# New positions for all tasks in a hand-planned attention and softplus kernel

## The chip, the cores and the metric

The kernel runs on one core of one Trainium2 chip. The metric is the device time of one execution in microseconds (us); the number given for a kernel is the median of its runs.

## The reference

Linear attention per head, a norm over each head's 64 values, and a two-layer network with softplus:

```python
# q, k, v: (8, 8, 576, 64)
kv = np.einsum('bhsd,bhse->bhde', k, v)
out = np.einsum('bhsd,bhde->bhse', q, kv)
rms = np.sqrt(np.mean(out * out, axis=-1, keepdims=True) + 1e-06)
x = out / rms * g_norm              # to 4608 tokens x 512
h = x @ w_in                        # 512 x 2048
g = np.maximum(h, 0.0) + np.log1p(np.exp(-np.abs(h)))
return g @ w_out                    # 2048 x 512, result 4608 x 512
```

The weights reach the kernel as 64-bit words and are converted on the chip.

## The kernel before, in words

Every large product is computed from three parts of each operand (a rounded main part, a scaled remainder and a correction), so one product of two 128-row tiles is three TensorE passes, all in the fp32r type.

The work has three stages that overlap:

- **Weights and attention.** The in and out weights come in 16 chunks of 128 hidden columns. Six VectorE and two ScalarE steps turn one 512 KB raw piece into fp32 (L434 to L464), and splitting into three parts takes two VectorE steps (L508 or L511, then L517) and three ScalarE steps (L501/L503, L514, L521). For the first four chunks the last VectorE step is replaced by two TensorE products, L525 and L526, with ScalarE's L529 behind. For each of the 8 batches, five groups of 64x64 products make the key-value matrix (L696), which ScalarE copies (L704). For each of 36 token tiles: the q tile is transposed (L776 and L783, later on VectorE, L751), multiplied with the key-value matrix (L720, 16 products of 64x64), squared (ScalarE L793), summed (VectorE L724), rooted (POOL L727 and L728), scaled (VectorE L732), transposed again (TensorE L738 and ScalarE L802 for the first 12 tiles) and stored to DRAM. The first six tiles are split at once (L640, L643, L646), the others are loaded again.
- **Narrow stage.** Blocks of 384 tokens go against single chunks: the first four blocks against 4 chunks, the other eight against 6. One step is 12 products L864, softplus and rounding on ScalarE (L886, L888), two VectorE steps (L875, L879) and nine products L871.
- **Wide stage.** Blocks of 512 tokens go against pairs of chunks by a scheme that needs seven instead of eight products of half size; each is six L1066. Softplus and rounding (L1094, L1124) and two VectorE steps (L1127, L1130) follow, then 24 products L1137. The token units for it are split by L1026, L1029, L1032.

Nothing of the order is written in the loops. Each piece of work is a task with an engine, a cost in ns, the tasks that it waits for, the buffers that it takes and gives, and a position. `Plan.order` replays all engines with these costs and, for each engine, picks the ready task with the lowest position among those that can start within 150 ns of the first:

```python
first = min(at for at, _ in options)
options = [(at, t) for at, t in options if at <= first + self.SOON]
...
at, t = min(options, key=lambda o: (o[1].pos, o[0]))
```

The result is the instruction order on every engine, SP's order of the loads and stores among them. On the chip each engine takes its list in order. Before the large products run, the plan sets dummy products (`warm`, L1232) into holes of TensorE's list of 400 ns or more.

The positions come from the loop indices plus the numbers of eight tables: `P0` (weights' conversion and fetch, attention's lead over the blocks), `P1` and `P2` (when weights are prepared for the wide stage, and when the later ones are fetched), `P3` (offsets inside a wide step), `P4` (each token tile), `P5` (each batch's key-value products and q loads), `P6` (units of the wide stage), `P7` (single loads of the first two batches). The planner's costs (`HANDOVER`, `SWITCH` and those given with each task) are not part of these tables.

## Time and profile before

| | before |
|---|---|
| median of 3 runs | 858.39 us (858.39 to 859.55) |
| profiled execution: span, first to last instruction | 856.4 us (its time outside the span is not listed) |
| TensorE busy | 843.0 us, 98% |
| VectorE busy | 704.1 us, 82% |
| ScalarE busy | 520.6 us, 61% |
| POOL busy | 76.6 us, 9% |
| granted TensorE clock | 1.00 |

PE is TensorE's matmul side, PEld its weight loads, DVE VectorE, ACT ScalarE, POOL GpSimd, SP the engine that issues the DMAs. A timeline row has start, length, engine, source line, operation, tiles, shape and count; rows of one kind that follow each other are merged, so a count of 32 for L720 is two tiles' half-passes: the profile lists each fp32 product L720 and L696 twice. Ends of matmuls are modelled and overlap with the next one's start, so lengths on TensorE are best taken from start to start. A bracket at the end of a row tells the idle time ahead of it and what ended it.

### The profile page before, as it was taken

Reading aid. Unit: us, or ns where it says so; the run is one execution under the profiler, and the core shown is the slowest. Engines: PE = TensorE matmul, PEld = TensorE weight load, DVE = VectorE, ACT = ScalarE, POOL = GpSimd, SP = SyncE. Lnnn points to the kernel's source line nnn. Section 1 sums busy time; section 2 is a strip of 40 time slices with the busy share of each in tenths; the row PEclk is TensorE's granted clock in tenths of the full one; section 3 lists DMA queues with packets and bytes.
Section 4 is the critical chain, followed back from the end, with each engine's and each line's share of the span. In section 5 each row is a group of like instructions: output and inputs, shape, how many; then the busy total and the mean of one; then the engine's idle time right before and its main releaser. Section 6 shows DMA issues by size and latency. Waiting matters only on the chain.

```text
span 856.4 us, 17075 instructions
## 1 busy us (share of the span) xinstructions
PE 843.0 (98%) x6464; PEld 754.1 (88%) x6464; DVE 704.1 (82%) x995; ACT 520.6 (61%) x980; POOL 76.6 (9%) x79
## 2 busy tenths in 40 slices
PE   8899999999999999999999999999999999999998
PEld 5578898999898999999999999998999899999996
DVE  7888898888788889798898788878788766788873
ACT  6766665446344567766667665655868555566654
POOL 0351223111113300000000000000000000000000
PEclk9999999999999999999999999999999999999999
DMA  9998997778884755436644546645364753777864
GB/s 283 297 233 212 261 273 232 185 245 218 214 188 119 194 160 185 142 110 207 210 156 154 180 151 206 195 158 181 124 197 138 234 168 102 240 237 246 249 189 131
DMA packets 239778, 167.07 MB, mean 195 GB/s; under 512 B 106320, under 2 KB 198736, under 8 KB 239696
## 3 DMA queue, kind: packets, MB, share of 16 engines
q1 hardware_dynamic: 239392, 165.86, 65.9%
q8 instruction: 50, 0.82, 0.4%
q14 instruction: 32, 0.26, 0.1%
q10 hardware_dynamic: 304, 0.13, 0.1%
HBM read 112.98 MB, written 52.95 MB: 194 GB/s over the span
## 4 chain that ended last, share of the span: by engine, by line
PE 94%; ACT 1%; DVE 1%; DMA 1%; issue 1%; POOL 0%; SPq 0%; POOLq 0%; DVEq 0%; ACTq 0%
PE banks L1137 31%; PE banks L1066 28%; PE banks L871 16%; PE banks L864 15%; PE banks L720 2%; PE banks L696 2%; DMA loads<-in_k_dram 1%; PE banks L738 0%; PE banks L1232 0%; PE banks L776 0%; DVE units L643 0%; DVE half L732 0%; DVE roots L724 0%; POOL roots L728 0%; ACT w L783 0%
## 5 line engine op out<-in xcount | busy, mean ns | idle before, releaser
L1137 PE MATMUL banks<-pieces,gv 128*128 128x512 f32 x768 | 236.8, 390 | 0.0
L1137 PE MATMUL banks<-pieces,g_False 128*128 128x512 f32 x384 | 149.4, 389 | 0.0
L1137 PEld LDWEIGHTS banks<-pieces,gv 128*128 128x128 f32 x768 | 132.5, 188 | 17.2 <-DVE banks L910 0.2
L864 PE MATMUL banks<-units,pieces 128*128 128x384 f32 x768 | 144.8, 337 | 0.0
L871 PE MATMUL banks<-pieces,gv 128*128 128x512 f32 x576 | 143.3, 393 | 0.0
L864 PEld LDWEIGHTS banks<-units,pieces 128*128 128x128 f32 x768 | 134.7, 188 | 4.5
L871 PEld LDWEIGHTS banks<-pieces,gv 128*128 128x128 f32 x576 | 106.2, 188 | 19.0
L1066 PEld LDWEIGHTS banks<-units,pieces 128*128 128x128 f32 x840 | 111.0, 188 | 6.5 <-ACT banks L1112 0.4
L1066 PE MATMUL banks<-units,pieces 128*128 128x256 f32 x840 | 115.2, 280 | 0.0
L886 ACT ACTIVATE half<-banks 128x384 f32<-128x384 f32 x64 | 31.4, 491 | 94.0 <-PE banks L864 90.7
L1127 DVE TENSOR_TENSOR gv<-g_True,gv 128x1024 fp32r<-128x1024 f32 x47 | 57.5, 1223 | 35.6 <-ACT gv L1124 35.5
L1137 PEld LDWEIGHTS banks<-pieces,g_False 128*128 128x128 f32 x384 | 72.1, 188 | 15.0
L1066 PEld LDWEIGHTS banks<-units,w 128*128 128x128 f32 x504 | 66.7, 188 | 3.7 <-ACT banks L1112 0.2
L1066 PE MATMUL banks<-units,w 128*128 128x256 f32 x504 | 69.6, 280 | 0.0
L728 POOL TENSOR_TENSOR roots<-roots,half 128x8 f32<-128x8 f32 x36 | 62.3, 1731 | 3.0
L1130 DVE SCALAR_TENSOR_TENSOR g_False<-gv 128x1024 fp32r<-128x1024 f32 x47 | 57.6, 1225 | 1.5
L1029 DVE TENSOR_TENSOR units<-loads,units 128x1024 fp32r<-128x1024 f32 x42 | 51.2, 1219 | 6.0 <-ACT units L1026 5.9
L1094 ACT ACTIVATE g_True<-banks 128x256 f32<-128x256 f32 x96 | 36.7, 384 | 30.6 <-PE banks L1066 29.9
L1116 DVE TENSOR_TENSOR g_True<-banks,g_True 128x512 f32<-128x512 f32 x48 | 33.1, 690 | 25.8 <-PE banks L1066 19.8
L931 ACT ACTIVATE m<-banks 128x512 f32<-128x512 f32 x72 | 42.1, 595 | 18.2 <-PE banks L1137 12.5
L1032 DVE SCALAR_TENSOR_TENSOR units<-units 128x1024 fp32r<-128x1024 f32 x42 | 51.4, 1224 | 1.7
L1026 ACT ACTIVATE units<-loads 128x1024 fp32r<-128x1024 f32 x42 | 44.3, 1056 | 12.4 <-PE banks L1066 10.1
(115 smaller groups left out, 1248.7 us busy)
## 6 DMA issues: line engine op xcount, KB each, us to landing
loads<-x SPq DMA_DIRECT2D x180, 128.0 KB, 2.7
part<-m SPq DMA_DIRECT2D x72, 256.0 KB, 3.1
m<-part SPq DMA_DIRECT2D x72, 256.0 KB, 3.4
loads<-form SPq DMA_DIRECT2D x45, 256.0 KB, 3.2
form<-loads SPq DMA_DIRECT2D x36, 256.0 KB, 3.0
raw<-in_moe_w_in_dram SPq DMA_DIRECT2D x16, 512.0 KB, 4.7
loads<-in_k_dram SPq DMA_DIRECT2D x32, 256.0 KB, 4.0
loads<-in_v_dram SPq DMA_DIRECT2D x32, 256.0 KB, 4.5
```

Of the source, the lines that this page charges most:

```text
L728: nc.gpsimd.tensor_tensor(out=r.tile, in0=r.tile, in1=half, op=ALU.pow)
L864: nc.tensor.matmul(from_the_end(hp, w), lhsT=w_in.tile[:, i, kd * P:(kd + 1) * P], rhs=from_the_end(xv.tile[:, i, kd], w), start=(m == 0), ...
L871: nc.tensor.matmul(mine[i].tile, lhsT=gv.tile[:, m, i * P:(i + 1) * P], rhs=w_out.tile[:, m], start=(c == cs[0] and m == 0), stop=(c == cs ...
L931: a = add("ACT", 690 if ph == LAST else 600, lambda: nc.scalar.activation(new(ot, [P, d_model]), bank.tile, func=AF.Copy, scale=scale if p ...
L1026: nc.scalar.activation(part_of(0, F32R), xl.tile if m > 1 else xl.tile[:, 0], func=AF.Copy, scale=DOWN)
L1029: nc.vector.tensor_tensor(out=part_of(1, F32R), in0=xl.tile if m > 1 else xl.tile[:, 0], in1=part_of(0), op=ALU.subtract)
L1032: nc.vector.scalar_tensor_tensor(out=part_of(2, F32R), in0=part_of(1), scalar=-RADIX, in1=part_of(0), op0=ALU.mult, op1=ALU.add)
L1066: nc.tensor.matmul(from_the_end(place(q), (16, 8)[kd]), lhsT=w[:, m, at:at + P], rhs=from_the_end(dst.tile[:, m, v, kd] if u < 6 else dst. ...
L1094: nc.scalar.activation(dst, src, func=AF.Softplus, scale=1.0 + E)
L1127: nc.vector.tensor_tensor(out=gvt(1, F32R), in0=gt(), in1=gvt(0), op=ALU.subtract)
L1130: nc.vector.scalar_tensor_tensor(out=gt(F32R), in0=gvt(1), scalar=-RADIX, in1=gvt(0), op0=ALU.mult, op1=ALU.add)
L1137: nc.tensor.matmul(from_the_end(mine[i].tile, P), lhsT=(gvt(m, F32R) if m < 2 else gt(F32R))[:, c, i * P:(i + 1) * P], rhs=from_the_end(ou ...
```

## The change

Only the numbers of the tables `P0` to `P7` change, in all eight of them. Work, tiles, buffers, dependencies and the planner's own costs stay; the counts of instructions stay, the 52 dummies aside, of which the changed order has 50. The tables' first and most changed lines:

```diff
-    P0 = [-45.94, -26.77, -11.8, 0.28, -29.91, -5.64, -2.86, 3.84, -103.4, -98.98, -69.3, -76.66, ...
+    P0 = [0.89, -0.01, 1.46, -0.06, -4.25, 1.41, 1.89, 3.82, -58.29, -56.6, -122.73, -98.51, ...
-    P4 = [-30.17, -6.08, 16.93, -33.9, -22.35, -28.91, -17.33, -7.12, -18.68, -2.69, 0.62, 2.73, ...
+    P4 = [-29.59, -15.99, -1.41, 3.77, -25.68, -50.78, -17.67, -31.7, -7.07, -4.44, -1.27, 0.31, ...
-    P5 = [1.24, -5.69, -2.28, -3.57, 1.72, 0.53, 6.68, -5.83, 3.01, -2.95, ...
+    P5 = [-5.58, -9.51, -1.52, 6.22, -6.19, -0.36, 4.02, 4.91, -67.3, 66.1, ...
-    P6 = [1.05, 6.24, 4.29, 4.08, -1.52, -2.85, 1.21, ...
+    P6 = [0.51, 6.21, 5.58, -2.87, 3.0, -4.45, -4.82, ...
-    P7 = [-23.78, -17.98, -11.85, -14.93, 0.41, 1.61, 7.35, 2.7, -25.02, -6.6, ...
+    P7 = [8.72, 8.67, 6.89, 4.99, 49.17, 7.84, 57.96, 55.49, 49.73, 47.43, ...
-    P1 = [49.11, 48.77, 51.0, 80.9, 122.61, 131.29, 2.87, 53.84, 71.21, 480.08, 304.47, 150.69]
+    P1 = [47.75, 47.43, 65.05, 68.87, 122.32, 131.27, 38.08, 53.44, 70.72, 132.08, 137.53, 139.18]
-    P2 = [24.08, 35.56, 23.68, 37.26, 50.08, 83.13, 74.26, 112.0, 102.25, 108.09, 139.38, -110.13, ...
+    P2 = [22.7, 35.98, 22.55, 37.01, 50.2, 78.32, 68.82, 107.05, 106.48, 100.06, 109.32, 1.36, ...
-    P3 = [2.14, 2.48, 6.41, -16.53, 0.86, 2.79, 4.01, -16.44, 3.79, 3.96, 2.19, 1.79, 0.72, 1.35, 1.55, -1.03]
+    P3 = [1.52, 2.23, 6.29, -2.38, 1.7, 4.2, 4.51, -0.5, 4.46, 1.69, 0.38, 2.05, 0.07, -2.36, 1.15, -1.15]
```

What becomes of it on TensorE, up to the first product L864 (the order of instructions, counts as issued; L696 and L720 are listed once here):

```
before: ... L776 x4, L525, L526, L1232 x4, L738 x4, L696 x16, L776 x4, L720 x16, L738 x4, L720 x16, L1232 x6, L864
after:  ... L776 x4, L1232 x3, L776 x8, L1232 x2, L696 x8, L738 x4, L696 x8, L525, L526, L720 x16, L776 x4, L864
```

More of the change, by code (lines that the diff above doesn't have):

```diff
@@ L258 @@
-    P6 = [1.05, 6.24, 4.29, 4.08, -1.52, -2.85, 1.21, -0.34, 3.11, 3.1, -1.07, -0.73, -0.88, 9.99, 5.7, 5.69, 0.13, 0.46]
-    P7 = [-23.78, -17.98, -11.85, -14.93, 0.41, 1.61, 7.35, 2.7, -25.02, -6.6, -15.2, -4.48, -2.14, 0.64, 2.93, 0.97, 4.67, 5.36, 3.33, 6.57, -10.37, 2.36, -14.11, -9.89, -7.11, 12.91, -2.89, 14.55, 12.59, 9.35]
+    P0 = [0.89, -0.01, 1.46, -0.06, -4.25, 1.41, 1.89, 3.82, -58.29, -56.6, -122.73, -98.51, -59.35, -4.74, -2.14, -3.52, 11.99, -48.72, 9.24, 9.64, 7.1, 37.25, -12.71, 4.2, 1.56, 10.37, -39.19, 5.42, 11.44, 2.02]
@@ new lines @@
+    P4 = [-29.59, -15.99, -1.41, 3.77, -25.68, -50.78, -17.67, -31.7, -7.07, -4.44, -1.27, 0.31, -73.43, -2.73, 1.39, 1.58, -0.37, 1.47, 1.42, 4.91, 13.94, 34.27, 0.4, 0.04, 4.43, 27.73, -26.03, -3.85, 9.5, 8.57, -5.79, -7.72, 3.62, 11.68, -32.58, -14.71]
+    P5 = [-5.58, -9.51, -1.52, 6.22, -6.19, -0.36, 4.02, 4.91, -67.3, 66.1, 4.13, 0.05, -7.34, -0.1, -8.38, -4.07]
+    P6 = [0.51, 6.21, 5.58, -2.87, 3.0, -4.45, -4.82, 0.71, 5.01, 6.69, 2.34, 5.68, 0.55, 8.39, 3.42, 9.26, 8.05, -0.07]
+    P7 = [8.72, 8.67, 6.89, 4.99, 49.17, 7.84, 57.96, 55.49, 49.73, 47.43, -15.1, -13.5, -0.35, -13.84, 28.74, 28.41, 28.53, 28.5, 32.0, 24.01, 24.26, -2.48, -16.92, -42.11, -13.08, 55.56, -23.84, 33.83, 9.34, 94.53]
@@ L264 @@
+    P2 = [22.7, 35.98, 22.55, 37.01, 50.2, 78.32, 68.82, 107.05, 106.48, 100.06, 109.32, 1.36, 107.7, 80.07, 109.43, 109.32, 110.04, 3.19, 142.41, 142.46, -7.39]
+    P3 = [1.52, 2.23, 6.29, -2.38, 1.7, 4.2, 4.51, -0.5, 4.46, 1.69, 0.38, 2.05, 0.07, -2.36, 1.15, -1.15]
     SPLIT = {p: (P1[i], P1[6 + i]) for i, p in enumerate((2, 3, 4, 5, 6, 7))}
```

4 lines of the change are left out of this document (removed).

## The prediction

> **What bounds the kernel now.** I read the page first: the engines' shares, then the chain that ended last.
>
> ```profile
> span 856.4 us, 17075 instructions
> ...
> PE 843.0 (98%) x6464; PEld 754.1 (88%) x6464; DVE 704.1 (82%) x995; ACT 520.6 (61%) x980; POOL 76.6 (9%) x79
> ...
> PE 94%; ACT 1%; DVE 1%; DMA 1%; issue 1%; POOL 0%; SPq 0%; POOLq 0%; DVEq 0%; ACTq 0%
> ```
>
> TensorE carries 94% of the chain, so a reordering can win only in what is not large product. The windows tell where that is (columns: stretch, its length, PE, weight loads, DVE, ACT, POOL, clock, DMA).
>
> ```profile
> 0.00:60.00 60.00, 50.50 (x657) 38.23 (x657) 50.74 (x89) 43.00 (x83) 17.63 (x23) 1.00 0.98 271
> 41.00:69.40 28.40, 26.47 (x321) 22.18 (x319) 25.41 (x45) 18.45 (x37) 11.00 (x10) 1.00 0.89 225
> 60.00:74.30 14.30, 14.19 (x170) 11.88 (x169) 12.43 (x23) 8.41 (x17) 4.06 (x4) 1.00 0.82 231
> 74.30:853.00 778.70, 778.33 (x5642) 703.94 (x5640) 640.46 (x884) 469.08 (x881) 54.87 (x53) 1.00 0.64 189
> 400.00:420.00 20.00, 20.00 (x129) 18.15 (x128) 18.39 (x23) 11.50 (x23) 0.00 (x0) 1.00 0.53 157
> ```
>
> From 74.30 us on TensorE misses 0.37 of 778.70 us. There the time is the work in its queue, and a new order can only change what the queue costs, or add waits. Ahead of 74.30 lies the filling: TensorE is 9.5 us idle in the first 60, and busy partly with L1232, the dummy products that the plan sets into holes. In those 60 us the DMA engines are busy 0.98 of the time and VectorE 50.74 us. So the change has two places to act: the filling, and the number of interruptions after it.
>
> **The end does not move by itself.** The last rows of the chain:
>
> ```profile
> 839.60 0.70 PE banks L1066 x6
> 840.30 0.68 PE banks L1137 x3
> ...
> 843.76 8.89 PE banks L1137 x39
> ```
>
> TensorE ends at 852.65; the remaining 3.75 us of the span (scaling and storing the last tile) follow on it in both versions, and both end their TensorE order with 39 L1137 in a row. The page gives the profiled execution's span, 856.4; the median of the runs is 858.39, so 2.0 us lie around the span. I add a difference to the median.
>
> **First part: the start of the large products.** The first L864 needs the three splits of token block 0, the third L646 on VectorE.
>
> ```profile
> 40.69 0.66 PE L738 MATMUL banks<-ident_r,half 128*128 128x128 f32 x4
> 41.97 0.69 PE L720 MATMUL banks<-early,w 64*64 64x64 f32 x32 [0.62 <-ACT half L793]
> 42.59 1.66 PE L1232 MATMUL banks<-ident_r 128*128 128x512 f32 x6
> 44.09 2.25 PE L864 MATMUL banks<-units,pieces 128*128 128x384 f32 x12
> ```
>
> ```profile
> 4.73 0.43 DVE L438 TENSOR_SCALAR m<-raw 128x512 uint32<-128x512 uint32 x1 [1.68 <-DMA raw<-in_moe_w_in_dram]
> ...
> 40.37 0.69 DVE L646 SCALAR_TENSOR_TENSOR units<-units 128x512 fp32r<-128x512 f32 x1
> ...
> 68.69 0.69 DVE L511 TENSOR_TENSOR m<-m,pieces 128x512 f32<-128x512 f32 x1
> ```
>
> The third L646 ends at 41.06, but TensorE's queue holds a transposition, an attention tile that waits 0.62 us and six dummies (1.50 us from 42.59 to 44.09, 0.25 each): 3.03 us lost. In the changed order the third L646 is again the 54th VectorE instruction from the first L438, with the same kinds ahead of it. On TensorE, behind the third L738, come only 8 L696, one L525/L526 pair, 16 L720 and 4 L776, with no dummy. The pair takes 0.75 (73.21 to 73.96 in a fence below), 16 L720 0.62 (264.96 to 265.58 below), the other two no more; all this lies beside the split of the third tile, a ScalarE step and two VectorE steps of 0.69 with VectorE's queue ahead of them. So the first L864 goes at about 41.1, some 3.0 us earlier. It does it with one attention tile fewer behind it (5 instead of 6) and one transposition fewer (3 instead of 4), which are then still to be done. SP's order ahead of this moves the first loads (both halves of the first two k/v pairs ahead of the first out weight, the fourth in weight behind the second batch's last k/v); the bytes ahead of the first batch's last k load are the same 4.9 MB, so I cost the DMA moves at nothing, covered by a DMA system that is full anyway; but 640 KB more stand ahead of the first out weight, 2.4 us at the 271 GB/s of the first window. VectorE has work on the first in weight meanwhile; I estimate that half of it shows there. Whether VectorE passes it on is a rival below.
>
> **Second part: the point at which both orders have done the same.** Starting earlier helps only if the rest of the filling keeps up. A good place to compare is the first L871 of the fourth chunk:
>
> ```profile
> 71.02 2.36 PE L864 MATMUL banks<-units,pieces 128*128 128x384 f32 x12
> 73.21 0.40 PE L525 MATMUL banks<-pieces,ident_r 128*128 128x512 f32 x1
> 73.45 0.40 PE L526 MATMUL banks<-pieces,gv 128*128 128x512 f32 x1
> 73.96 0.50 PE L1232 MATMUL banks<-ident_r 128*128 128x512 f32 x1
> 74.30 1.55 PE L871 MATMUL banks<-pieces,gv 128*128 128x512 f32 x6
> ```
>
> Counted in both orders, TensorE has by then done the same: 5 groups of L864, 27 L871, 11 attention tiles, 9 transpositions, three batches of k/v products, all 8 L525 pairs, and all dummies. It is reached at 74.30 now. When in the changed order? TensorE's own work from the first L864 to this point is 30.5 us there: 16.6 of large products (5 x 2.09 and 27 x 0.227, prices from the third part), six attention tiles at 0.47, six visits at 0.39, and about 8.8 (estimates of 0.25 to 0.55 each by the rows shown) for six transpositions, five k/v groups, a q tile, three pairs and six dummies. So not before 41.2 + 30.5 = 71.7. VectorE's side: the fourth out weight must be split, and that L511, which ends at 69.38 now, moves from the 97th to the 100th VectorE instruction. With the same idle time VectorE would end it 1.6 us later (about three instructions of 0.5 to 0.7), at 71.0; then L514, the L525/L526 pair (0.75) and L529 follow; for the two ScalarE steps with their handovers I estimate 0.65 to 0.7 each, as for VectorE's 0.69 on the same 512 columns: 2.1 us, so 73.1. VectorE idled 2.99 of the 28.40 us between 41.0 and 69.4, partly because TensorE was late, so some of the 1.6 comes back. Bounds: 71.7 (TensorE's own work) and 75.9 (now, plus 1.6). I take 73.0, near VectorE's row, since this stage follows VectorE: **1.3 us earlier**.
>
> **Third part: what is left after that point.** The large products are the same. The small ones are the same too: 25 attention tiles, 3 transpositions, five batches of k/v, no dummies. What differs is in how many visits they are done: 16 now, 19 in the changed order (tiles 12 to 19 stand more often alone). The price of a visit:
>
> ```profile
> 107.78 2.25 PE L864 MATMUL banks<-units,pieces 128*128 128x384 f32 x12
> 109.96 1.16 PE L720 MATMUL banks<-early,w 64*64 64x64 f32 x64
> 111.05 4.39 PE L871 MATMUL banks<-pieces,gv 128*128 128x512 f32 x18
> 115.28 2.25 PE L864 MATMUL banks<-units,pieces 128*128 128x384 f32 x12
> ...
> 262.78 2.25 PE L864 MATMUL banks<-units,pieces 128*128 128x384 f32 x12
> 264.96 0.69 PE L720 MATMUL banks<-early,w 64*64 64x64 f32 x32
> 265.58 2.35 PE L871 MATMUL banks<-pieces,gv 128*128 128x512 f32 x9
> 267.77 2.25 PE L864 MATMUL banks<-units,pieces 128*128 128x384 f32 x12
> 269.86 2.20 PE L871 MATMUL banks<-pieces,gv 128*128 128x512 f32 x9
> ```
>
> By starts: 12 L864 take 2.09 (267.77 to 269.86); an L871 takes 0.227 (0.68 for three, above). A visit of two tiles lengthens 107.78 to 115.28 by 7.50 - 2.09 - 4.08 = 1.33; a visit of one lengthens 262.78 to 267.77 by 4.99 - 2.09 - 2.04 = 0.86. So a tile costs 0.47 and the visit itself 0.39. Three visits more cost **1.2 us**; one visit fewer holds both kinds, and one transposition now lies inside a visit, which I put at 0.1 together: 1.1. [...]
>
> In this stage a wait could also appear anew. The gated groups (L871 behind L879, L864 behind L646) stand at about the same distance from their producers; the third, sixth, ninth and twelfth L646 stand at VectorE's places 54, the same, or earlier than before (128 for 133, 158 for 167). The stage from 115 to 330 us has the same visits in the same places. I cost new waits there at nothing, bounded by one wide VectorE instruction, 1.2 us (last row shown), in front of a needed one.
>
> **Fourth part: the wide stage.** Both orders hold the same 2016 L1066 and 1152 L1137. The order is mostly the same pattern; where it differs is the first four steps, and of these step 3 loses cover. Between the last product of step 3 and its first L1137 there stood four products and five L1137 triples, 4 x 0.70 + 5 x 0.68 = 6.2 us; now two products and five triples, 4.8 us. What must fit in:
>
> ```profile
> 388.74 0.39 ACT L1094 ACTIVATE g_True<-banks 128x256 f32<-128x256 f32 x1 [0.32 <-PE banks L1066]
> ```
>
> ```profile
> 391.50 1.22 DVE L1130 SCALAR_TENSOR_TENSOR g_False<-gv 128x1024 fp32r<-128x1024 f32 x1
> ```
>
> That chain took 392.72 - 388.74 = 4.0 us. So 0.8 us are left, and later steps ran without a wait on the same 4.8 in the before kernel. I take nothing.
>
> **The sum.** 74.30 to 73.0: -1.3; visits: +1.1; waits: 0. Together -0.2 us: 858.39 - 0.2 = 858.2. That is no change that could be told: about 0.2%, 1.7 us, is what a measurement of this kernel separates from none.
>
> **The rivals.** *The filling closes up* (0.31). VectorE's 2.99 idle us were TensorE's doing, and vanish with the earlier start; then the common point comes at 71.7, or near 71 if the loads also land earlier: -2.6 to -3.3, +1.1 for visits: -1.5 to -2.2, 856.2. For it: six dummies and a wait stood ahead of a ready product. Against it: the last split of the filling moved back three places, and VectorE was already 90% busy there.
>
> *The wide stage stalls* (0.22), the case on the slow side. In 400 to 420 VectorE is busy 18.39 of 20 us, and one of its wide instructions takes 1.22. Where such an instruction stands ahead of L1127 in a step with 4.8 us of cover, 4.0 + 1.2 is 0.4 too long, and two of them 1.6. The preparation of weights is spread anew by `P1` and `P2`: counted in both orders by VectorE's lengths, 1.3 us more work stands ahead of the fourth and eleventh L1130, measured against TensorE's place, and 2.4 us more ahead of the thirteenth (estimates). It decides from two stalls of 1.2 on; three give +3.6 - 0.2: 861.8. For it: VectorE has 8% to spare there. Against it: its other work can slide, and the steady steps showed no wait.
>
> *The start is not earlier* (0.11). If the first out weight lands 1.2 us later and VectorE, in order, passes this on, the common point comes at 74.2 to 75.9, and the visits come on top: +1.0 to +2.7, about 860.3.
>
> **Chances and range.** No change (856.7 to 860.1) 0.36, the largest single case; faster 0.31; slower 0.33, from the two slow rivals. The range reaches from the faster rival's lower end with 0.6 us for the start (855.6) to three stalls (861.8).
>
> **What would show it.** In the changed profile: first L864 near 41.1, not 44; the first L871 of the fourth chunk near 73; no PE wait after it; 19 visits from there, each 0.39 plus tiles; TensorE's end near 852.5. It is wrong if the waits view shows L1137 behind L1130 in 360 to 420, if the common point lies outside 71.7 to 75.9, or if the first L864 comes after 43.

## The result, and the profile after

The changed kernel takes 861.28 us, the median of 10 runs (860.31 to 866.38). The kernel before took 858.39 us on the same chip (10 runs, 857.51 to 860.97). The ratio is 1.0037, with a 95% interval of 1.0023 to 1.0051, so it is slower by 2.9 us where the prediction's central case was no change. The time is inside the range given. What came is close to the rival that was given 0.11, *the start is not earlier* (about 860.3). By its own signs the prediction is wrong at one point: the first L864 came at 43.14, after the 43 that it had named.

The profiled execution took 861.22 us, near the median. Its page, the same three lines as for the kernel before:

```profile
span 859.4 us, 17059 instructions
...
PE 844.1 (98%) x6462; PEld 754.9 (88%) x6462; DVE 702.1 (82%) x995; ACT 519.1 (60%) x980; POOL 74.7 (9%) x79
...
PE 94%; DMA 1%; ACT 1%; DVE 1%; POOL 1%; issue 0%; SPq 0%; DVEq 0%; ACTq 0%
```

The shares tell nothing: TensorE carries 94% of the chain in both. The 3.0 us of span must be looked for at the points that the prediction named. TensorE's timeline around the first L864, and around the common point, the first L871 of the fourth chunk:

```profile
42.73 0.66 PE L776 MATMUL banks<-ident_r,w 128*128 128x128 f32 x4 [0.41 <-DVE units L643]
43.14 1.13 PE L864 MATMUL banks<-units,pieces 128*128 128x384 f32 x5
```

```profile
75.50 2.63 PE L871 MATMUL banks<-pieces,gv 128*128 128x512 f32 x9
77.97 2.25 PE L864 MATMUL banks<-units,pieces 128*128 128x384 f32 x12
80.06 0.60 PE L738 MATMUL banks<-ident_r,half 128*128 128x128 f32 x4
80.42 0.95 PE L871 MATMUL banks<-pieces,gv 128*128 128x512 f32 x3
82.13 0.66 PE L738 MATMUL banks<-ident_r,half 128*128 128x128 f32 x4 [0.77 <-ACT w L802]
```

The first L864 comes at 43.14 (forecast 41.1, before 44.09), the common point at 75.50 (forecast 73.0, before 74.30). Behind it stands a wait of 0.77 us that the kernel before did not have. The first L1066 of the wide stage, of the kernel before and then of the changed one:

```profile
336.24 0.88 PE L1066 MATMUL banks<-early,pieces 128*128 128x256 f32 x6
```

```profile
339.55 0.88 PE L1066 MATMUL banks<-early,pieces 128*128 128x256 f32 x6
```

From common point to L1066 it is 261.94 us before and 264.05 after. So the account is: +1.20 up to the common point, +2.11 from there to the wide stage, and from there to the end 519.85 for 520.16, -0.31. Together +3.0, the difference of the spans.

**Why the start is late.** VectorE's timeline after:

```profile
8.13 0.69 DVE L464 TENSOR_TENSOR m<-m,m 128x512 f32<-128x512 f32 x1
11.19 0.43 DVE L438 TENSOR_SCALAR m<-g 128x512 uint32<-128x512 uint32 x1 [2.37 <-DMA g<-in_moe_w_out_dram]
...
17.28 0.69 DVE L447 SCALAR_TENSOR_TENSOR m<-sq,m 128x512 f32<-128x512 bf16 x1 [0.50 <-ACT sq L434]
...
25.07 1.28 DVE L724 TENSOR_REDUCE roots<-half 128x8 f32<-128x512 f32 x2 [0.27 <-ACT half L793]
...
42.71 0.69 DVE L646 SCALAR_TENSOR_TENSOR units<-units 128x512 fp32r<-128x512 f32 x1
```

and the two rows of the kernel before that answer to the second and the fourth:

```profile
8.53 0.42 DVE L438 TENSOR_SCALAR m<-g 128x512 uint32<-128x512 uint32 x1
...
22.83 1.28 DVE L724 TENSOR_REDUCE roots<-half 128x8 f32<-128x512 f32 x2 [0.48 <-ACT half L793]
```

The first out weight landed at 11.16 instead of 7.62, and VectorE, which takes its list in order, began its second conversion at 11.19 instead of 8.53. At the first L724, the first step that needs an attention tile, it is 2.24 us late, and at the third L646 2.34 (42.71 for 40.37). That the first L864 is still 0.95 us earlier is the three microseconds of queue that the new order took away in front of it.

TensorE had a stall of its own at the same time. Its timeline, and the windows (columns as in the prediction: the last three are clock, DMA share, GB/s) of the changed kernel:

```profile
9.47 1.98 PE L696 MATMUL banks<-loads 128*64 128x64 f32 x32 [3.75 <-DMA loads<-in_k_dram]
11.37 2.50 PE L1232 MATMUL banks<-ident_r 128*128 128x512 f32 x5
```

```profile
7.00:12.00 5.00, 2.53 (x34) 2.35 (x35) 2.53 (x5) 2.15 (x4) 0.24 (x1) 0.59 1.01 304
12.00:16.00 4.00, 4.00 (x17) 3.10 (x16) 3.79 (x7) 1.40 (x3) 0.00 (x0) 0.66 1.00 303
```

It waits 3.75 us for a k load that now stands behind three other loads of k and v, and behind the gap the granted clock is 0.59 and 0.66 (1.00 in the same windows before). Five dummies take 2.30 us from start to start, 0.46 each, where the prediction's row gave 0.25.

The chain that ended last in the changed kernel, followed through its first 45 us, does not pass through the out weight. Its two pieces of DMA are k loads:

```profile
2.77 6.56 DMA loads<-in_k_dram
...
28.80 5.96 DMA loads<-in_k_dram
```

The first is the load that TensorE waits 3.75 us for. From there the chain goes through TensorE and ScalarE to the square L793 that the first L724 waits for, and VectorE, which had waited for the out weight, is ready for that L724 only 0.27 us before it. So two chains are late there by nearly the same amount, and the out weight is on the one that ends first.

### The profile page after: what moved, and what is told of

The parts are those of the page before. It is cut to its first block, busy times and chain, and to the rows that moved or that the text cites. A ratio compares the mean times of both kernels' runs of the same rounds, so it can differ in the third digit from the quotient of the medians.

```text
span 859.4 us, 17059 instructions
## 1 busy us (share of the span) xinstructions
PE 844.1 (98%) x6462; PEld 754.9 (88%) x6462; DVE 702.1 (82%) x995; ACT 519.1 (60%) x980; POOL 74.7 (9%) x79
## 4 chain that ended last, share of the span: by engine, by line
PE 94%; DMA 1%; ACT 1%; DVE 1%; POOL 1%; issue 0%; SPq 0%; DVEq 0%; ACTq 0%
PE banks L1137 30%; PE banks L1066 27%; PE banks L864 15%; PE banks L871 15%; PE banks L696 2%; PE banks L720 2%; DMA loads<-in_k_dram 1%; PE banks L1232 1%; POOL roots L728 0%; PE banks L738 0%; PE banks L776 0%; ACT half L793 0%; DVE half L732 0%; ACT w L802 0%; DVE units L643 0%
## 5 line engine op out<-in xcount | busy, mean ns | idle before, releaser
L1137 PE MATMUL banks<-pieces,gv 128*128 128x512 f32 x768 | 236.8, 389 | 0.0
L1137 PE MATMUL banks<-pieces,g_False 128*128 128x512 f32 x384 | 149.4, 389 | 0.0
L1137 PEld LDWEIGHTS banks<-pieces,gv 128*128 128x128 f32 x768 | 132.9, 188 | 17.7 <-DVE banks L910 0.2
L864 PE MATMUL banks<-units,pieces 128*128 128x384 f32 x768 | 145.5, 337 | 0.0
L871 PE MATMUL banks<-pieces,gv 128*128 128x512 f32 x576 | 143.6, 393 | 0.1
L864 PEld LDWEIGHTS banks<-units,pieces 128*128 128x128 f32 x768 | 134.4, 188 | 4.6
L871 PEld LDWEIGHTS banks<-pieces,gv 128*128 128x128 f32 x576 | 106.0, 188 | 19.6 <-ACT pieces L529 0.6
L1066 PEld LDWEIGHTS banks<-units,pieces 128*128 128x128 f32 x840 | 111.0, 188 | 6.1
L1066 PE MATMUL banks<-units,pieces 128*128 128x256 f32 x840 | 114.9, 280 | 0.0
L1137 PEld LDWEIGHTS banks<-pieces,g_False 128*128 128x128 f32 x384 | 72.1, 188 | 15.2
L1066 PEld LDWEIGHTS banks<-units,w 128*128 128x128 f32 x504 | 66.6, 188 | 3.7
L1066 PE MATMUL banks<-units,w 128*128 128x256 f32 x504 | 69.0, 280 | 0.0
L1112 ACT COPY banks<-banks 128x256 f32<-128x256 f32 x48 | 17.3, 360 | 59.9 <-PE banks L1066 59.7
```

Source lines behind the costliest of these rows:

```text
L864: nc.tensor.matmul(from_the_end(hp, w), lhsT=w_in.tile[:, i, kd * P:(kd + 1) * P], rhs=from_the_end(xv.tile[:, i, kd], w), start=(m == 0), ...
L871: nc.tensor.matmul(mine[i].tile, lhsT=gv.tile[:, m, i * P:(i + 1) * P], rhs=w_out.tile[:, m], start=(c == cs[0] and m == 0), stop=(c == cs ...
L1066: nc.tensor.matmul(from_the_end(place(q), (16, 8)[kd]), lhsT=w[:, m, at:at + P], rhs=from_the_end(dst.tile[:, m, v, kd] if u < 6 else dst. ...
L1137: nc.tensor.matmul(from_the_end(mine[i].tile, P), lhsT=(gvt(m, F32R) if m < 2 else gt(F32R))[:, c, i * P:(i + 1) * P], rhs=from_the_end(ou ...
```

## The experiments

Each kernel was timed beside the kernel before on the same chip; ratios are to that. Kernels named as edits of an order change no computation: only the sequence of the instructions on the engines named. The common point means the first L871 of the fourth chunk throughout.

### Is it the first out weight? Is it the clock? What does a visit cost?

Three theories stood at first: VectorE passes on the late out weight; TensorE's lower clock behind its gap (0.59 and 0.66) delays the rest; and the visits behind the common point cost 0.39 us each.

**e1: the changed kernel, out weight moved forward.**

```diff
 SP:  L423 in weight,
+     L423 out weight,
      L685 v, L685 k, L685 v, L685 k,
-     L423 out weight,
      L683 v, ...
```

> The changed kernel with one DMA issue moved on SP: the first out weight (512 KB) is loaded right behind the first in weight, ahead of the first four k/v loads (1 MB). All other engines keep the changed order. VectorE theory (the late landing of this weight, 11.16 us instead of 7.62, made VectorE idle 2.4 us ahead of its second conversion, and VectorE, in order, passed this on to the first L864 and to the common point): second conversion at about 8.8 instead of 11.2, first L864 at about 41 instead of 43.1, total 1.2 to 2.4 us less, 859 to 860. Theory of the waits view (TensorE's longest wait, 3.75 us for a k load, is what costs): the k loads land about 1.8 us later still, so the total is the same or up to 1.8 us more, 861.3 to 863. Theory that only the visits and waits after the common point cost: no change, 861.3.

Measured: 863.92 us, ratio 1.0048 (1.0035 to 1.0060). The wait for the out weight is gone, and this stands in its place on VectorE:

```profile
18.20 0.69 DVE L447 SCALAR_TENSOR_TENSOR m<-sq,m 128x512 f32<-128x512 bf16 x1 [2.62 <-ACT sq L434]
```

With the out weight ahead, the k loads land later (10.35 for 9.33), the q transpositions on TensorE come later, ScalarE waits for these with two L783 (up to 4.3 us) and only then takes the square L434 that VectorE needs. The first L864 comes at 44.05. So the out weight's load is not the cause by itself. (The profiled execution took 862.03 us, among the fast ones of e1. The interval overlaps that of the changed kernel, so it is not shown that e1 is slower than that.)

**e2: the kernel before, out weight moved back.** The converse, in the other order:

```diff
 SP:  L423 in weight, L685 k, L683 k,
-     L423 out weight,
      L685 v, L685 v, L685 k,
+     L423 out weight,
      L766 q, ...
```

> The kernel before with one DMA issue moved on SP: the first out weight is loaded behind the first four k/v loads and the first k tail instead of ahead of three of them. VectorE theory: its second conversion starts at about 10.8 instead of 8.5, the first L864 at 45 to 46.4 instead of 44.1 and the common point at 75.5 to 76.6 instead of 74.3: 859.6 to 860.7. Other theories: within 0.5 us of the kernel before, 858.4, since k and v land earlier and TensorE waits less for them.

Measured: 862.07 us, ratio 1.0029 (1.0017 to 1.0041).

```profile
11.73 0.43 DVE L438 TENSOR_SCALAR m<-g 128x512 uint32<-128x512 uint32 x1 [3.49 <-DMA g<-in_moe_w_out_dram]
```

This one move of a load makes the kernel before slower by most of what the whole change did (1.0029 and 1.0037). A load moved past others is not free here: that is shown. In its profiled execution, which was at the slow end of its runs, the first L864 came at 49.65, later than the 3.49 us alone explain; the granted clock was 0.50 from 16 to 20 us there. The clock alone is not the reason: the execution with the highest mean granted clock, 0.999, still took 861.77 us.

**e3: the kernel before with more visits.** Eight attention tiles behind the common point are done in two halves, with an L871 triple between them:

```diff
-            t.run()
+            t.run(range(2))          # half of the tile's L720
+            by_id[halves_at[id(t)]].run()   # the next L871 triple
+            t.run(range(2, NP))      # the other half
```

> The kernel before with eight of the later attention tiles done in two halves, an L871 triple between them: same work, eight more visits to small products. If a visit costs 0.39 us as worked out from the rows: plus 3.1 us, 861.5. [...]

Measured: 861.34 us, ratio 1.0029 (1.0018 to 1.0040).

```profile
74.32 1.56 PE L871 MATMUL banks<-pieces,gv 128*128 128x512 f32 x6
```

```profile
339.12 0.88 PE L1066 MATMUL banks<-early,pieces 128*128 128x256 f32 x6
```

From common point to L1066 264.80 us instead of 261.94: 2.86 us for eight visits, 0.36 each, with the same work. The price of a visit holds.

**e6: the changed kernel kept warm.** Nine more dummies ahead of the first k/v product:

```diff
 PE:  L1232 x11,
+     L1232 x9,
      L696 (first k/v products), ...
```

> The changed kernel with nine more dummy products ahead of the first k/v visit, so that TensorE does not idle 3.75 us there and its clock stays up (in the changed kernel's profile the dummies behind that wait take 0.43 us each, those of the kernel before 0.25). If the clock in the filling costs: about 1 to 1.5 us less, 860. VectorE theory: TensorE is not what the filling waits for, so no change, 861.3 within 0.5.

Measured: 862.51 us, ratio 1.0042 (1.0030 to 1.0055). The clock is 1.00 in every window from 0 to 44 us, and the first L724 still comes at 25.34, the first L864 at 43.41. With the clock at 1.00, TensorE waits 1.35 us for the next k load instead, at 17.28. The clock of 0.59 and 0.66 from 7 to 16 us is not what made the start late.

### Both at once, and the two halves exchanged

**e7: e1, and eight dummies left out** between the first k/v products and the second q transposition.

```diff
 PE:  L696 (first k/v products),
-     L1232 x5,
      L776 x4,
-     L1232 x3,
      L776 x4, ...
```

> The changed kernel with its first out weight loaded right behind the first in weight, and without the eight dummy matmuls that stand between the first k/v products and the second q transposition on TensorE (they took 0.43 us each). Two-chain theory (the first L864 is set by the later of two chains, VectorE behind the first out weight and TensorE behind the second k load, whose late q transpositions hold up ScalarE): the wait of 2.62 us of L447 for ScalarE in the run with the weight alone moved shrinks by 1 us or more, the first L864 comes at 41.4 to 42.5 instead of 44.05, and the time is 1.5 to 2.5 us under that run and 0 to 1 us under the changed kernel. Single-chain theory (VectorE behind the loads alone): the first L864 stays at 43.5 to 44.1, the time within 0.6 us of the run with the weight alone moved.

Measured: 862.53 us, ratio 1.0047 (1.0030 to 1.0065). L447's wait shrank from 2.62 to 0.76 as the two-chain theory had it, but VectorE then waits for the next weight:

```profile
21.11 0.43 DVE L438 TENSOR_SCALAR m<-g 128x512 uint32<-128x512 uint32 x1 [2.00 <-DMA g<-in_moe_w_out_dram]
```

The first L864 comes at 44.35. The gain of the two-chain theory did not come. The time is that of e1, as the single-chain theory had it, but the wait that makes it is another.

**e9: the kernel before without the six dummies ahead of its first L864.**

```diff
 PE:  L738 x4, L720 (a tile),
-     L1232 x6,
      L864, ...
```

> The kernel before without the six dummy matmuls that stand right ahead of its first L864. They took 0.25 us each in its trace. If the dummies stand on the path (TensorE in order): the first L864 up to 1.5 us earlier, 42.6 to 44.1, and the time 0 to 1.5 us lower. If they only fill a wait for the out weight's halves: no change, the first L864 at 44.1, the time within 0.3 us. If the cold clock then costs more than the dummies: up to 1 us slower.

Measured: 858.61 us, ratio 0.9999 (0.9990 to 1.0008), no change. The first L864 goes 0.93 us earlier, at 43.16, and the common point stays, at 74.74 for 74.30. That group of L864 then stops after eight of its twelve products, 0.45 us for an L646. The profiled execution had also begun late (first L724 at 23.71 for 22.83, behind a wait of 0.99 us for the second in weight), so its 0.44 us at the common point say little. By the ratio, these dummies were not on the path to the common point in the order before, where VectorE came no earlier. This says nothing of an order in which VectorE comes earlier too.

**e11 and e12: old start with new rest, new start with old rest.** The order of one kernel up to the common point and of the other behind it, on all engines; tasks that the first had already done are skipped in the second:

```diff
-    for t in plan.order():
+    for t in forced(plan, SEQ):   # SEQ: one order's list up to the cut, then the other's
```

> The order of the kernel before up to the first L871 of the fourth chunk, on every engine, and of the changed kernel behind it: the same set of TensorE work stands ahead of that point in both. Theory of parts: that point stays at 74.3, three more visits at 0.39 us and the new wait of 0.77 us come behind it: 1.9 to 2.1 us slower than the kernel before, ratio about 1.0023. Rival (the late start is all, and the visits close up): no change from the kernel before, within 0.5 us.

> The order of the changed kernel up to the first L871 of the fourth chunk, on every engine, and of the kernel before behind it. Theory of parts: that point at 75.5 instead of 74.3, and the same work behind it as before: 1.0 to 1.4 us slower than the kernel before, ratio about 1.0014. Rival (the visits behind that point are all): no change, within 0.5 us. If both hybrids are slower and their differences add up to the changed kernel's 3 us, the two parts are independent.

Measured: e11 869.61 us, ratio 1.0121 (1.0107 to 1.0135); e12 866.16 us, ratio 1.0080 (1.0065 to 1.0095). Both are slower than either kernel, since the seam stalls. In e11 ScalarE and, behind it, TensorE:

```profile
85.85 0.60 ACT L931 ACTIVATE m<-banks 128x512 f32<-128x512 f32 x1 [9.63 <-DMA part<-m]
```

```profile
88.85 1.11 PE L738 MATMUL banks<-ident_r,half 128*128 128x128 f32 x4 [8.65 <-ACT w L802]
```

and in e12:

```profile
82.97 1.12 PE L696 MATMUL banks<-loads 128*64 128x64 f32 x16 [4.92 <-DMA loads<-in_v_dram]
```

TensorE had done the same work at the cut in both orders, but SP had not: a store or a load that the new half counts on came late. As a division of the 3 us these two are inconclusive.

### Where it lies, and whether the parts can be undone

**e20 and e21: the same exchange at a later cut,** the first L871 of the eighteenth chunk (146.92 us before, 150.32 after), where only one VectorE instruction is done in one order and not in the other.

> The order of the kernel before up to the first L871 of the eighteenth chunk (146.92 us in its trace, 150.32 in the changed kernel's), on every engine, and of the changed kernel behind it. At this point the two orders have the same work behind them on every engine but for one VectorE instruction. If the whole difference comes ahead of that point (3.4 us of it does by the two traces): the time of the kernel before, within 0.3 us. If the wide stage of the changed kernel brings anything of its own: the difference shows here.

> The converse: the order of the changed kernel up to the first L871 of the eighteenth chunk, and of the kernel before behind it. If the whole difference comes ahead of that point: the time of the changed kernel, 2.5 to 3.5 us over the kernel before, ratio 1.003 to 1.004. If the wide stage shares in it: less.

Measured: old front with new rest 859.13 us, ratio 1.0006 (0.9995 to 1.0017), the time of the kernel before. New front with old rest 862.81 us, ratio 1.0051 (1.0037 to 1.0066), slower like the changed kernel (above the 1.003 to 1.004 expected, with an interval that overlaps it). So the whole loss arises ahead of that point, and the wide stage has no share in it.

**e13: other load order.** Two loads instead of four ahead of the first out weight, and the pair first that TensorE takes first:

```diff
 SP:  L423 in weight,
-     L685 v1, L685 k1, L685 v0, L685 k0, L423 out weight,
+     L685 v0, L685 k0, L423 out weight, L685 v1, L685 k1,
```

> The changed kernel with its first loads in another order, all else as it was: first in weight, v and k of the first pair, first out weight, v and k of the second pair (it had v and k of the second pair, of the first pair, and then the out weight). It puts two loads instead of four ahead of the first out weight, and the pair that TensorE takes first ahead of the other. Theory of the load order (the start is late by what stands ahead of two items in the queue): first out weight at 8 to 9 instead of 11.16, TensorE's wait of 3.75 us down to 2.5 or less, granted clock nearer full at 7 to 16 us, first L864 at 41.5 to 42.5 instead of 43.14, time 0.7 to 1.7 us under the changed kernel's 861.3. Rival (the queues are full at 300 GB/s to 24 us, and the next weight comes late in place of the first): VectorE's idle time moves to the second in weight or the second out weight, first L864 at 43 or later, time within 0.5 us of the changed kernel.

Measured: 862.21 us, ratio 1.0048 (1.0036 to 1.0060). The out weight landed at 8.62 and TensorE's longest wait fell to 2.5 us, as the load-order theory had it, and the first L864 came at 45.86, as it had not. VectorE waited 2.4 us for the square L434 as in e1. Also, its profiled execution (864.46 us) shows clock 0.66 from 36 to 40 us.

**e15: the changed kernel with three visits merged** with their neighbours. One of the three is a lone transposition, so of the 19 visits with attention tiles or k/v products 17 are left, where the kernel before has 16:

```diff
-PE:  L864 x12, L738 x4, L871 x3, L738 x4, L720 (a tile), L871 x6
+PE:  L864 x12, L871 x9, L738 x4, L738 x4, L720 (a tile)
 ...
-     L720 (a tile), L864 x12, L720 (a tile)
+     L864 x12, L720 (a tile), L720 (a tile)
 ...
-     L720 (a tile), L864 x12, L696, L720 (a tile)
+     L864 x12, L720 (a tile), L696, L720 (a tile)
```

> The changed kernel with three visits of small products merged with the next one: three L871 triples go ahead of the L738 that waited 0.77 us for ScalarE's L802, and two attention tiles go behind the L864 that followed them, next to the products there. 16 visits behind the common point instead of 19, as in the kernel before. Theory of parts: 3 x 0.39 us less, and the 0.77 us wait gone or hidden: 1.2 to 1.9 us under the changed kernel (859.4 to 860.1 against 861.3), the common point unchanged at 75.5. Rival (the visits cost nothing of their own, the delay is all in the start): no change from the changed kernel, within 0.4 us. If the moved tiles come late for their users: slower than the changed kernel, with a new wait of L864 or L720.

Measured: 864.84 us, ratio 1.0082 (1.0062 to 1.0103): slower than the changed kernel, the third case of the expectation. From common point (75.85) to the first L1066 (343.49) it is 267.64 us, 3.6 more than in the changed kernel. Of the waits view, by the form "waiting line <- releaser: us in all, times, longest", first e15, then the changed kernel:

```profile
PE banks L720 <- DVE half L732: 1.8, 2, 1.5
...
PE banks L720 <- ACT w L802: 1.2, 2, 0.8
```

```profile
PE banks L720 <- ACT w L802: 0.5, 1, 0.5
...
PE banks L720 <- DVE half L732: 0.3, 1, 0.3
```

Two tiles in a row wait for VectorE and ScalarE to free what the first has used. In the changed order large products stand between these tiles, and 0.5 and 0.3 us of such waits are left. That a visit saved is worth the 0.36 to 0.39 us of one added, no run shows.

**e16: e13 and e15 together.**

> Both edits together: the changed kernel with the other order of its first loads and with the three visits merged. If both parts are right and independent, their gains add: 1.9 to 3.6 us under the changed kernel, that is 857.7 to 859.4 where the kernel before is at 859, level with it or up to 1.3 us faster. If only the visits count: 859.4 to 860.1.

Measured: 865.08 us, ratio 1.0081 (1.0067 to 1.0095), as e15 alone. Nothing adds up, because neither part gained.

**e18 and e19: the square ahead.** e13, and ScalarE's square of the second in weight ahead of the two copies that it queued behind; e19 leaves out the eight dummies of e7 too.

```diff
 ACT: L451,
+     L434 (second in weight),
      L783, L783,
-     L434 (second in weight),
      L503, ...
```

> The changed kernel with the other order of its first loads and, on ScalarE, the square of the second in weight (L434) moved ahead of the two copies of the q transpositions (L783) that it was queued behind. Theory (ScalarE is in order, and what it waits for in those copies is passed on to VectorE): L447's wait for L434 of 2.2 to 2.4 us goes, VectorE goes on at about 15.8, the first L864 comes at 41.2 to 42.3, the common point (first L871 of the fourth chunk) at 73.5 to 74.7, and the time is 0.8 to 2.0 us under the changed kernel's 861.3. Rival (the loads themselves bind): VectorE waits 2 us for the second out weight instead, the first L864 stays at 43 or later, and the time within 0.5 us of the changed kernel.

> The run with the square ahead, and without the eight dummies between the first k/v products and the second q transposition. If ScalarE's copies and the clock no longer stand on VectorE's path, the same as that run within 0.5 us; if the copies still do, up to 1 us faster; if the second out weight lands late as in the run that only lacked the dummies, 1 us slower.

Measured: e18 862.30 us, ratio 1.0046 (1.0033 to 1.0059); e19 863.72 us, ratio 1.0056 (1.0044 to 1.0068). In e18 VectorE's wait is gone at L447, and back at L724:

```profile
15.63 0.69 DVE L447 SCALAR_TENSOR_TENSOR m<-sq,m 128x512 f32<-128x512 bf16 x1
...
24.93 1.28 DVE L724 TENSOR_REDUCE roots<-half 128x8 f32<-128x512 f32 x2 [0.86 <-ACT half L793]
```

VectorE is through its four conversions 0.74 us earlier than in the changed kernel and then waits for the attention tile, which TensorE begins at 23.07 (23.22 in the changed kernel, 20.97 before). In e19 VectorE waits 3.2 us for an L501 that stands behind another copy on ScalarE, and L724 comes at 27.42. So at the first L724 two chains arrive within a microsecond of each other, and each of them runs through two or three in-order queues.

**e22, e23, e24: several queues at once.** e22 is e18 with two L525/L526 pairs behind the first two attention tiles instead of ahead of them, their L529 likewise, one L501 ahead of an L529, and six dummies fewer. e23 adds ten dummies in TensorE's first two gaps. e24 also moves a v and a k load ahead of the fourth out weight:

```diff
 PE:  L696 (third product), L525, L526,
-     L1232 x6, L696, L525, L526, L696, L525, L526, L720 (two tiles)
+     L696, L696, L720 (two tiles), L525, L526, L525, L526          # e22
 PE:  L1232 x11,
+     L1232 x4,                                                      # e23
      L696 (first product),
+     L1232 x6,                                                      # e23
      L696 (second product), ...
 SP:
+     L685 v, L685 k,                                                # e24
      L683 v, L423 fourth out weight,
-     L685 v, L685 k,                                                # e24
```

> The run with the square ahead, and besides: on TensorE the two L525/L526 pairs that stand ahead of the first two attention tiles (1.27 us each with the k/v product between them) go behind those tiles, and the six dummies ahead of the third k/v product are left out; on ScalarE the L529 copies that go with the pairs go behind the tiles' copies, and one L501 goes ahead of an L529. Theory (three in-order queues reach the first L724 within 1 us of each other, so one at a time brings nothing): first L720 at 21.0 to 21.9 instead of 23.07, first L724 at 23.0 to 24.1 instead of 24.93, first L864 at 42.0 to 43.0, common point at 74.3 to 75.2, time 0.4 to 1.5 us under the changed kernel's 861.3. Rival (the loads bind): the third k/v product still starts after 20 us, the first L720 at 22.5 or later, the first L864 at 43.3 or later, no gain.

> The run with the three queues, and ten more dummies in TensorE's two gaps: four ahead of the first k/v product and six ahead of the second. In the profile of the run without them the granted clock stood at 0.50 from 12 to 16 us and again at 0.67 and 0.50 from 36 to 44, and the third L643 waited 2.66 us for ScalarE. Theory (that run lost its gain to the clock): clock 1.00 to 44 us, first L724 at 24.0 or earlier, first L864 at 42.0 to 43.0, common point at 74.3 to 75.2, time 860.0 to 861.0. Rival (the gain is not there even at the full clock): first L864 at 43.4 or later, common point at 75.8 or later, time 861.3 or more.

> The run with the queues and the warm-up, and on the load queue the v and k load of the seventh k/v product (issued at 28.39 and 28.84, landed at 35.46 and 36.03 there) moved ahead of the fourth out weight (issued at 27.75, landed at 34.81) and of the v tail in front of it. In that run TensorE waited 2.48 us for this k load at 36.16, and the granted clock fell to 0.74 and 0.50 from 36 to 44. Theory (the load queue is full to 36 us, and its order is what binds; the clock loss follows from the gap): k lands at 31 to 33, the gap closes, the clock stays at 1.00 to 44 us, first L864 at 41.8 to 43.0, common point at 74.2 to 75.3, time 860.0 to 861.0. Rival (VectorE's own work, or the out weight that now lands 1 us later, binds): first L864 at 43.2 or later, common point at 75.6 or later, time 861.3 or more.

Measured: e22 863.62 us, ratio 1.0050 (1.0036 to 1.0064); e23 862.46, 1.0042 (1.0027 to 1.0057); e24 863.76, 1.0044 (1.0028 to 1.0060). The first L724 does come earlier in e22 (24.41) and e23 (23.70, within 0.9 us of the kernel before), so the queues were part of what held it; in e24, with the same queues, it comes at 25.42, with a granted clock of 0.67 from 16 to 20 us. The gain does not reach the first L864: 45.61, 46.09, 46.20. On e22's VectorE the last split of the first block waits, and in the windows of e23 and then e24 the clock has fallen by that time:

```profile
44.45 0.69 DVE L643 TENSOR_TENSOR units<-banks,units 128x512 fp32r<-128x512 f32 x1 [2.66 <-ACT w L802]
```

```profile
36.00:40.00 4.00, 3.84 (x32) 3.06 (x33) 3.03 (x6) 1.39 (x5) 1.90 (x2) 0.74 0.88 246
40.00:44.00 4.00, 4.00 (x39) 2.78 (x38) 2.20 (x4) 1.22 (x3) 0.00 (x0) 0.50 1.05 303
```

```profile
36.00:40.00 4.00, 3.25 (x16) 2.30 (x17) 3.74 (x8) 2.13 (x5) 2.74 (x3) 0.73 0.84 250
40.00:44.00 4.00, 4.00 (x38) 2.82 (x38) 2.32 (x4) 1.33 (x3) 0.00 (x0) 0.50 1.05 283
```

In e23 TensorE's gap ahead of it was a wait of 2.48 us for a k load behind the fourth out weight (landed at 36.03 and 34.81). In e24 that wait is 0.34:

```profile
34.88 0.69 PE L696 MATMUL banks<-loads 128*64 128x64 f32 x16 [0.34 <-DMA loads<-in_k_dram]
```

and the clock falls all the same. So the theory that the k load's gap causes it falls too. These profiled executions are slower than their medians for e22 and e24 by 0.5 and 0.9 us and for e23 by 1.95 us, so the loss at 36 to 44 us is probably not in every run. But the executions of the three with a mean granted clock of 1.00 took 861.08, 862.92 and 861.75 us, and the changed kernel's own begin at 860.31: no gain is seen at the full clock either.

## Why the prediction was wrong, step by step

**First part: the mechanism right, one term mis-sized.** The first L864 does follow the third L646 directly now; that removed 3 us of queue. The step that failed is the sentence that costs the moved loads at nothing, "covered by a DMA system that is full anyway". The same bytes ahead did not mean the same time: the k load that the 4.9 MB were counted for was issued at 14.78 instead of 12.59 and landed 5.0 us after its issue instead of 5.9, so about 1.3 us late. Nor was the DMA system full where it mattered. From 4 to 5 and from 5 to 6 us its share was 0.70 and 0.44 (200 and 81 GB/s; 1.01 and 1.05 before, 293 and 270 GB/s), while SP waited 1.3 us ahead of the v load L683 and the out weight had not landed. The 0.98 of the prediction is a mean over 60 us. The out weight landed 3.54 us later (11.16 for 7.62), where the prediction had estimated 2.4 with half of it showing, and had left even this to a rival. VectorE was idle 2.37 us for it, and the third L646 is 2.34 us late. That the load order has a price of this size is shown by e2, in the other kernel. That undoing it does not bring the time back is shown by e1 and e13: TensorE's k and q products and ScalarE's copies are late for loads as well, and reach the first L724 within a microsecond of VectorE. The prediction followed VectorE alone; it did not look at what TensorE and ScalarE wait for ahead of 25 us, with k, v and q loads in another order.

**Second part: 73.0 forecast, 75.50 came, and most of the miss is the first part's.** The bounds 71.7 to 75.9 hold it. From the first L864 to the common point 31.9 us were forecast (73.0 less 41.1) and 32.36 came; TensorE was busy for 30.58 of them, as the 30.5 of own work had it. This distance hardly varies. In the changed kernel, e1, e6, e7, e13, e15, e16, e18, e19 and e22 to e24 it is 32.35 to 32.37 us, with the first L864 anywhere from 43.14 to 46.20, and from the common point to the first L1066 it is 264.01 to 264.06 us in all of these but e15 and e16, whose visits are merged. So whatever these kernels did to the start of the changed order arrived undiminished at the wide stage: here the start counts in full. The way over VectorE was half right. The fourth out weight's split is the row

```profile
72.88 0.69 DVE L511 TENSOR_TENSOR m<-m,pieces 128x512 f32<-128x512 f32 x1
```

It begins 4.19 us later than before, where 1.6 were forecast. VectorE had worked 1.58 us more by then, as forecast, but it had idled 9.25 us instead of 6.83, and "the same idle time" was the assumption; the late start is most of that. From the end of L511 to the common point it took 1.93 us (2.1 forecast). TensorE's own queue reaches L525 at 74.48 without a listed wait, so whether it or VectorE came last there is not shown. (Two small slips in the working: the 41.2 in 41.2 + 30.5 stands for the 41.1 just forecast, and the 0.68 for three L871 is read from a row of L1137.)

**Third part: the visits as forecast, one wait not seen.** Three more visits at 0.39 are 1.17; e3 gives 0.36 a visit. The rest of the 2.11 us is the wait of 0.77 us of L738 for L802 and 0.2 of small differences. New waits had been costed at nothing with a bound of 1.2, and 0.77 lies within it. The price held, though not as a saving: e15 merged three visits and came out 3.6 us longer, with new waits. What TensorE does in the 0.36 to 0.39 us of a visit added, no run shows; e3, with the same tiles in eight more visits, shows that they go with the visit and not with the tile.

**Fourth part: right.** The wide stage took 519.85 us for 520.16, and e20, whose wide stage is the changed one, is as fast as the kernel before. The rival *the wide stage stalls* did not come.

**The miss, added up.** Against the forecast, in the span: the first L864 is 2.04 us late (43.14 for 41.1), the stretch to the common point 0.46 longer, the stretch to the wide stage 1.01 more than the 1.1 for visits, and the rest 0.31 shorter. That is 3.2 us, from -0.2 to +3.0, and two thirds of it is the start.

**The chances.** That the time lies inside the range is luck: the upper end, 861.8, was put there for three stalls of the wide stage, and none came. *The start is not earlier* was described with the right place and nearly the right sum (+1.0 to +2.7; it was +3.0 in span), and was given the smallest chance, because the bytes ahead of the last k load were counted and not the bytes ahead of each item that an engine waits for first.

**What stays open.** Which single edit, if any, would give the changed order the start of the kernel before: nine kernels took away waits that stood out, and the first L864 came between 43.4 and 46.2 in all of them. No kernel was tried with the whole load order of the kernel before. A sum fits nine profiles within 0.1 us (the changed kernel, e1, e6, e7, e12, e15, e16, e19, e21; clock 1.00 from 24 to 44 us in each): the first L864 comes at the later of two times, the first L724 plus 18.06 us, and the product L696 behind the k load that the changed kernel issues at 28.80, plus 7.37 us (25.07 and 34.89 in the changed kernel: 43.13 and 42.26). e18 is 0.83 above it, with one more wait of 0.77 us for a k load. By this estimate the forecast 41.1 needed the first L724 at 23.0 and that product at 33.7, both at once. The sum is fitted to these profiles and no run tests it. Open is also what makes the granted clock fall at 36 to 44 us in some executions. None of the kernels tried beats the kernel before; e9 and e20 are level with it.

## What to carry to other kernels

Where several engines wait for one load queue, moving a load was a trade between them here (in e1 the wait of 2.37 us for the out weight went, and one of 2.62 us for L434 came): for every consumer, count the bytes ahead of the first item that it waits for, not the bytes of the whole start, and read the queue's share in that stretch (0.70 and 0.44 from 4 to 6 us in the changed kernel), not over 60 us (0.98 in the kernel before). Look for the point behind which the distances stay the same from kernel to kernel (264.01 to 264.06 us here): what was lost ahead of it was not won back here. Where several in-order queues met at one instruction with less than a microsecond between them, taking away the wait that the profile names brought the next one into its place (2.62 us in e1, 2.00 in e7, 0.86 in e18); a forecast has to follow all of them to that point. And the price of an added interruption (0.36 us in e3) is not the gain of a removed one (three merged in e15 made the stretch 3.6 us longer): what had been put in between may have been covering a wait.

## What was not expected of the hardware

The granted TensorE clock fell behind gaps of very different length, and not in every execution: 0.59 and 0.66 in the changed kernel's windows from 7 to 16 us behind a gap of 3.75 us, and 0.50 from 40 to 44 us in e24, where no wait above 0.61 us stood in the eight microseconds ahead. The kernel before kept 1.00 with a gap of 1.08 us and several of 0.5 in the same stretch, and e16 kept 1.00 in every window from 7 to 44 us with waits for k loads of up to 2.2 us. With nine more dummies in the gap of 3.75 us it stayed at 1.00 (e6). So a lower clock was seen behind short waits once and not another time, and no run tells what decides it.

Two orders that have the same TensorE work behind them could not be joined at 75 us without 5 to 9 us of stall on TensorE (8.65 in e11, 4.92 in e12); joined at 147 us they lost nothing (e20, whose first L1066 comes at 335.70, 336.24 before). At 75 us seven of SP's tasks, four of VectorE's and one of ScalarE's were done in one order and not in the other, at 147 us one of VectorE's; the stalls were all behind loads and stores.
